# All engines in program order, by unit; integer additions and first own terms on VectorE; round 1's transposes between levels

## The chip, the cores and the metric

One core of one Trainium2 chip. The metric is the device time of one execution in microseconds (us); quoted are medians of all the runs of a kernel, at first with the lowest and highest. One caution on names: SyncE issues the loads, GpSimd appears as POOL in the profile, ScalarE as ACT, VectorE as DVE, TensorE as PE and its weight loads as PEld.

## The reference

A recurrence over 768 time steps for 4 batches and 8 heads of 48 channels, then a normed two-layer MLP with a residual:

```python
for t in range(S):                                   # S = 768, B = 4, H = 8, D = 48
    cur = einsum('bhd,bhe->bhde', u[None] * kt, vt)  # the step's "own term"
    y[:, :, t] = einsum('bhd,bhde->bhe', rt, state + cur)
    state = wt[..., None] * state + einsum('bhd,bhe->bhde', kt, vt)
x  = y transposed to (B, S, H*D)                      # 384 channels
xn = (x - mu) / sqrt(var + 1e-6) * g_ln
out = x + relu(xn @ w_ch1) @ w_ch2                    # 384 -> 1536 -> 384
```

The two weight matrices arrive as 64-bit words and are made into 32-bit floats on the chip.

## The kernel before

The work is cut into eight **rounds** (a batch and half its steps), each of two **units** (four heads). A round's recurrence is done in six **levels**: TensorE makes products (`a_ps`, the quads), VectorE multiplies `r` and `k` by the decays (grow) and keeps blocks under a mask. The MLP of a round runs in 24 steps, spread over the levels of the rounds after it. A level of round 1 or later, with its share of MLP steps, is called a **slot**; slots 0 to 7 are round 1 and two levels of round 2.

The 24 blocks of weights are converted one at a time. ScalarE reads the fetched block twice, VectorE runs three integer instructions and GpSimd adds:

```python
PE, ACT, DVE, POOL, SP = nc.tensor, nc.scalar, nc.vector, nc.gpsimd, nc.sync
def matmul(*args, **kw):                     # only TensorE's order is fixed
    tc.keep_in_program_order(PE.matmul(*args, **kw))

def weights():
    ...
    for i, (dst, _) in enumerate(parts):     # 24 blocks, 3 raw buffers
        fetch(i + 2)                         # SyncE loads 384 KB
        ...
        ACT.activation(out=e.bitcast(F32), in_=hi.bitcast(F32), func=AF.Abs, scale=2.0**-16)
        ACT.activation(out=low, in_=lo, func=AF.Copy, scale=2.0**-29)
        DVE.tensor_scalar(...)               # clamp
        DVE.tensor_scalar(...)               # shift and mask
        DVE.scalar_tensor_tensor(...)        # sign
        POOL.tensor_tensor(out=dst.bitcast(I32), in0=e, in1=low, op=ALU.add)
        yield
```

ScalarE has a second duty: it takes the transposes (`wT`, `kT`, `rT`, `kn`, `xT`) and the MLP's Relu (`h`) out of PSUM, and TensorE waits for it whenever a PSUM buffer is full (two for each of these two kinds). Outside TensorE a scheduler decides where each instruction stands in its engine's queue. The driver:

```python
for rnd in range(1, NR + 1):
    for lev in range(NLEV):
        ...
        if now: level(now, lev)              # quads, grow, keep
        tasks = []                           # transposes of round rnd + 1, ...
        ...
        fill(until, tasks)                   # tasks mixed with the MLP's steps
        ...
        convert(3)                           # three weight blocks a slot, after the slot
```

## Time and profile before

| | before |
|---|---|
| time | 634.4 us, median of 3 (631.36 to 634.47) |
| profiled span | 628.1 us |
| first MLP matmul (`h_ps`) | 85.4 us |
| end of slot 7 | 150.4 us |
| TensorE busy in slots 0 to 7 | 59.45 of 65.0 us, granted clock 0.91 |
| the rest of the span | 477.7 us, TensorE busy 466.16 |

Two lines of the view of waits, cut to 64 to 151 us, matter for what follows. In this view a line names the engine and tile that waited, what it waited for, then the total in us, how often and the longest. These are ScalarE's waits at the two instructions that open a weight block:

```profile
ACT wl L212 <- POOL w_sb L225: 5.5, 1, 5.5
ACT we L209 <- DMA raw<-in_moe_w_ch_dram: 5.1, 6, 1.1
```

On these two lines ScalarE stands for 10.6 us at weight blocks in some 87 us, half of it in one piece for GpSimd's addition; the waits for loads are 1.1 us at the longest. (Ahead of 64 us it waits 21.2 us more for weight loads, before the MLP has begun.)

### The profile page before, as it was taken

What the parts mean: (1) busy time and instruction counts of PE and PEld (TensorE: products, weight loads), DVE (VectorE), ACT (ScalarE), POOL (GpSimd) and SP (SyncE); (2) the same over time, 40 slices, a digit from 0 to 9 for tenths busy, and PEclk for the clock granted to TensorE, in tenths of its full rate; (3) what the DMA queues carried; (4) which work ended last, traced back from release to release, by engine and by line L of the source; (5) the groups of instructions that cost most, each with busy time, mean ns of one, the idle gap of its engine ahead of it and who ended that gap; (6) DMA issues with size and microseconds to landing.
All of it is one profiled execution on the core that took longest, in us unless ns stands there. A gap on an engine that the chain in (4) does not pass through costs nothing.

```text
span 628.1 us, 19238 instructions
## 1 busy us (share of the span) xinstructions
PE 573.4 (91%) x8456; PEld 387.2 (62%) x8456; DVE 303.2 (48%) x683; ACT 185.2 (29%) x402; POOL 152.4 (24%) x205
## 2 busy tenths in 40 slices
PE   5366597989999999999999999999999999999997
PEld 4255465656656766667667666676666666566554
DVE  1598959867563544452646356355226361231000
ACT  4108426352143311531243213331142004301200
POOL 7666737670160013300330005101030000000000
PEclk9556769889999989999999999998999999999999
DMA  7656766803410342013400341002000000000000
GB/s 134 144 105 190 182 124 175 183 14 77 91 48 1 59 94 47 15 39 74 88 15 12 68 99 38 1 16 46 26 15 3 15 15 14 1 15 25 1 13 25
DMA packets 123251, 36.83 MB, mean 59 GB/s; under 512 B 116896, under 2 KB 120096, under 8 KB 123168
## 3 DMA queue, kind: packets, MB, share of 16 engines
q1 hardware_dynamic: 121568, 35.32, 25.4%
q8 instruction: 66, 1.08, 0.7%
q10 hardware_dynamic: 1600, 0.30, 0.3%
q14 instruction: 17, 0.14, 0.1%
HBM read 30.87 MB, written 4.72 MB: 57 GB/s over the span
## 4 chain that ended last, share of the span: by engine, by line
PE 82%; DVE 8%; issue 3%; DMA 2%; POOL 2%; SPq 2%; ACT 1%; POOLq 0%; DVEq 0%; ACTq 0%
PE h_ps L56 30%; PE o_ps L56 29%; PE a_ps L56 10%; PE y L56 4%; PE kv L56 2%; PE r_ps L59 2%; PE kn_ps L59 2%; SPq L112 2%; DVE we L221 1%; PE w_ps L59 1%; PE xT_ps L59 1%; DMA nat_r<-in_r_dram 1%; DVE kT L309 1%; PE k_ps L59 1%; DVE rT L309 1%
## 5 line engine op out<-in xcount | busy, mean ns | idle before, releaser
L56 PE MATMUL h_ps<-xT,w_sb 128*128 128x384 f32 x576 | 202.1, 499 | 2.2 <-ACT h L475 2.2
L56 PE MATMUL o_ps<-w_sb,h 128*128 128x384 f32 x576 | 201.2, 495 | 0.0
L56 PEld LDWEIGHTS h_ps<-xT,w_sb 128*128 128x128 f32 x576 | 107.3, 194 | 66.5 <-issue 4.2
L56 PEld LDWEIGHTS o_ps<-w_sb,h 128*128 128x128 f32 x576 | 106.4, 194 | 61.3 <-issue 3.0
L56 PE MATMUL a_ps<-rT,kT 48*64 48x32 f32 x4608 | 86.8, 229 | 25.8 <-DVE kT L309 20.2
L56 PEld LDWEIGHTS a_ps<-rT,kT 48*64 48x64 f32 x4608 | 81.2, 146 | 37.4 <-issue 19.7
L475 ACT ACTIVATE h<-h_ps 128x384 f32<-128x384 f32 x96 | 47.0, 489 | 114.6 <-PE h_ps L56 111.7
L487 DVE TENSOR_TENSOR o<-o_ps,x 128x384 f32<-128x384 f32 x24 | 13.3, 556 | 118.3 <-PE o_ps L56 118.3
L280 POOL TENSOR_TENSOR vo<-v,own 128x576 f32<-128x576 f32 x16 | 19.5, 1221 | 196.1 <-DMA v<-in_v_dram 123.9
L309 DVE TENSOR_TENSOR kT<-kT,tot 128x384 f32<-128x384 f32 x80 | 60.2, 752 | 0.0
L323 DVE COPY_PREDICATED A<-mask,a_ps 128x384 f32<-128x384 int8 x80 | 54.6, 751 | 0.0
L309 DVE TENSOR_TENSOR rT<-rT,tot 128x384 f32<-128x384 f32 x80 | 49.9, 623 | 4.3 <-PE a_ps L56 2.1
L374 DVE SCALAR_TENSOR_TENSOR s<-s,decay,kv 128x48 f32<-128x48 f32 x160 | 30.4, 258 | 43.7 <-PE kv L56 43.7
L421 DVE TENSOR_TENSOR x<-y,vo 128x576 f32<-128x576 f32 x16 | 12.1, 757 | 61.6 <-PE y L56 61.6
L225 POOL TENSOR_TENSOR w_sb<-we,wl 128x384 int32<-128x384 int32 x24 | 33.7, 1416 | 25.6 <-DVE we L221 22.5
L264 POOL TENSOR_TENSOR rk<-nat_k,nat_r 128x576 f32<-128x576 f32 x16 | 27.1, 1691 | 36.1 <-DMA nat_r<-in_r_dram 17.3
L275 DVE TENSOR_REDUCE own<-rk 128x12 f32<-128x576 f32 x16 | 12.0, 749 | 46.5 <-POOL rk L269 46.5
L460 ACT ACTIVATE xT<-xT_ps,g_sb 128x384 f32<-128x384 f32 x24 | 13.9, 580 | 58.5 <-PE xT_ps L59 58.5
L241 ACT COPY rT<-r_ps 128x384 f32<-128x384 f32 x32 | 14.6, 477 | 50.7 <-PE r_ps L59 50.7
L241 ACT COPY kT<-k_ps 128x384 f32<-128x384 f32 x32 | 14.8, 478 | 43.9 <-PE k_ps L59 43.8
L56 PEld LDWEIGHTS y<-v,A 64*64 64x64 f32 x384 | 21.8, 138 | 8.1 <-issue 7.1
L255 POOL TENSOR_TENSOR tot<-wT 128x384 f32<-128x384 f32 x16 | 14.6, 911 | 46.9 <-DVE kT L309 46.8
(57 smaller groups left out, 591.1 us busy)
## 6 DMA issues: line engine op xcount, KB each, us to landing
raw<-in_moe_w_ch_dram SPq DMA_DIRECT2D x24, 384.0 KB, 3.7
nat_w<-in_w_dram SPq DMA_DIRECT2D x64, 72.0 KB, 2.5
nat_k<-in_k_dram SPq DMA_DIRECT2D x64, 72.0 KB, 2.5
v<-in_v_dram SPq DMA_DIRECT2D x64, 72.0 KB, 2.8
out_dram<-o SPq DMA_DIRECT2D x24, 192.0 KB, 2.0
nat_r<-in_r_dram SPq DMA_DIRECT2D x60, 72.0 KB, 2.4
vx<-in_v_dram SPq DMA_DIRECT2D x64, 36.0 KB, 2.3
nat_r<-in_r_dram ACTq DMA_DIRECT2D x4, 72.0 KB, 3.7
```

The source lines that it names most:

```text
L56: tc.keep_in_program_order(PE.matmul(*args, **kw))
L59: tc.keep_in_program_order(PE.transpose(*args))
L225: POOL.tensor_tensor(out=dst.bitcast(I32), in0=e, in1=low, op=ALU.add)
L241: ACT.copy(out=a[nm][:, ts(pr, RN)], in_=ps)
L255: POOL.tensor_tensor(out=t, in0=pair[:, :, 0], in1=pair[:, :, 1], op=ALU.mult)
L264: POOL.tensor_tensor(out=rk, in0=nat["k"][q % 2][:, :, :, 0:D], in1=nat["r"][q % 2][:, :, :, 0:D], op=ALU.mult,)
L280: POOL.tensor_tensor(out=a["vo"], in0=vn[q], in1=o[:, :, :, None].broadcast_to([P, NH, TT, D]), op=ALU.mult,)
L309: DVE.tensor_tensor(out=X, in0=X, in1=T[:, :, 1 - i][:, :, None].broadcast_to(blocks), op=ALU.mult,)
L323: DVE.copy_predicated(out=out_j[:, :, :, 1, :], mask=mask, data=ps_j)
L374: DVE.scalar_tensor_tensor(out=s[:, pr, m, :], in0=s[:, pr, m - 1, :] if m else before[:, pr, 2 * TT - 1, :], scalar=a["T"][NLEV][:, c : c ...
L460: ACT.activation(out=xTs[rnd][:, kc, :], in_=ps, func=AF.Copy, scale=g_sb[:, kc : kc + 1])
L475: ACT.activation(out=hs[f], in_=ps, func=AF.Relu)
```

## The change

Its intent: let VectorE do what GpSimd slowed it for, start VectorE on unit 0 as soon as that unit has arrived, use TensorE's idle prologue for round 1's transposes, and fix every order by hand, so that the tuned order is what runs. The core of the diff:

```diff
+class InOrder:                       # every call is kept in program order
+    def __getattr__(self, name):
+        ...
+        return lambda *args, **kw: self.tc.keep_in_program_order(f(*args, **kw))
-    PE, ACT, DVE, POOL, SP = nc.tensor, nc.scalar, nc.vector, nc.gpsimd, nc.sync
+    PE, ACT, DVE, POOL = (
+        InOrder(tc, e) for e in (nc.tensor, nc.scalar, nc.vector, nc.gpsimd)
+    )
+    SP = nc.sync
...
+    praw = ctx.enter_context(tc.tile_pool(name="praw", bufs=4))
+    RAW = 4
+    def begin():                         # "opening": ScalarE, needs raw[i] and a low buffer
+        ...
+            low[i] = p3.tile([P, WC], I32, tag="low", name=f"low{i}")     # 3 buffers
+            ACT.activation(out=parts[i][0], in_=hi.bitcast(F32), func=AF.Abs, scale=2.0**-16)
+            ACT.activation(out=low[i], in_=lo, func=AF.Copy, scale=2.0**-29)
+    def join():                          # VectorE, then the freed raw buffer is loaded again
+        ...
-            POOL.tensor_tensor(out=dst.bitcast(I32), in0=e, in1=low, op=ALU.add)
+            DVE.tensor_tensor(out=bits, in0=bits, in1=low.pop(i), op=ALU.add)
+            joined = i + 1
+            fetch()
...
+    for lev in range(1, NLEV):           # round 0
+        for q in (u0, u1):
+            quads(q, lev)
+        if lev > 1:
+            run(ahead[3 * lev - 6 : 3 * lev - 3])     # round 1's transposes
...
+    states(u1)
+    begin()
+    begin()
+    exchanged(u1)
...
+    PARTS = (2, 2, 2, 3, 3, 3, 3, 3)
...
+            if slot < len(PARTS):
+                for _ in range(PARTS[slot]):
+                    tasks += [join, begin]            # ahead of the slot's transposes
...
+            fill(until, tasks)
```

An **opening** is ScalarE's two reads of a block, into the weight tile and a `low` buffer; a **join** is VectorE's four instructions that finish the block, after which its raw buffer is loaded again. The own terms of the first four units and their products of decays (`totals`) go to VectorE, and VectorE's copies of `x` before the norm are gone. At the start of the MLP six blocks are open and three joined.

## The prediction

> **What bounds the kernel now.** I read the page's slices first, then the busy times in three windows of my own, the groups by line, and the timeline of VectorE. The slices show two regimes. In the first five or so of 40, TensorE is about half busy and its granted clock is low; from about the ninth on it is 90% busy or more at a clock of 0.8 to 1.0.
>
> ```profile
> PE   5366597989999999999999999999999999999997
> DVE  1598959867563544452646356355226361231000
> PEclk9556769889999989999999999998999999999999
> ```
>
> The windows put numbers on it. I cut at 85.40 us, where the first MLP matmul (`h_ps`) starts, and at 150.40, where the second level of round 2 ends. Columns: length, then busy time of PE, PEld, DVE, ACT, POOL, then clock and DMA.
>
> ```profile
> 0.00:85.40 85.40, 47.81 (x1038) 39.45 (x1038) 58.31 (x119) 33.31 (x70) 55.33 (x87) 0.67 0.68 151
> 85.40:150.40 65.00, 59.45 (x930) 39.73 (x930) 51.15 (x104) 30.32 (x68) 36.38 (x32) 0.91 0.48 111
> 150.40:628.10 477.70, 466.16 (x6490) 308.01 (x6489) 193.70 (x460) 121.54 (x264) 60.70 (x86) 0.99 0.16 35
> ```
>
> The last 477.7 us have 11.5 us of idle TensorE, and 3.4 of those belong to the tail after 560 us. Its work is the same in both kernels, so little can be won there. Of the first 85.4 us TensorE is idle for 37.6. From 25 to 50 us VectorE was busy for all 25.00 us: it is the bound of the prologue (round 0, before the first MLP). In the middle window TensorE lacks 5.5 us. So a change of the schedule can move only two dates: when the first MLP starts, and when TensorE reaches the end of the eighth slot. A slot is one level of rounds 1 and later with its share of MLP steps; slots 0 to 7 are round 1 and two levels of round 2. At the end of slot 7 both kernels have issued 17 of the 24 steps of the first MLP, since the formula for the steps is the same.
>
> The groups show what makes VectorE slow:
>
> ```profile
> L225 POOL TENSOR_TENSOR w_sb<-we,wl 128x384 int32<-128x384 int32 x24 | 33.7, 1416 | 25.6 <-DVE we L221 22.5
> L309 DVE TENSOR_TENSOR kT<-kT,tot 128x384 f32<-128x384 f32 x80 | 60.2, 752 | 0.0
> L323 DVE COPY_PREDICATED A<-mask,a_ps 128x384 f32<-128x384 int8 x80 | 54.6, 751 | 0.0
> ```
>
> and the timeline of VectorE, then of GpSimd, shows the same instruction at two speeds:
>
> ```profile
> 54.50 0.36 DVE L217 TENSOR_SCALAR we<-we 128x384 int32<-128x384 int32 x1
> 54.90 0.56 DVE L221 SCALAR_TENSOR_TENSOR we<-raw,we 128x384 int32<-128x384 int32 x1
> 57.83 1.00 DVE L217 TENSOR_SCALAR we<-we 128x384 int32<-128x384 int32 x1
> 57.60 1.00 POOL L225 TENSOR_TENSOR w_sb<-we,wl 128x384 int32<-128x384 int32 x1 [1.00 <-DVE we L221]
> ```
>
> L217 takes 0.36 us alone and 1.00 beside GpSimd's addition.
>
> **What the Trainium skill says.** "GPSIMD Engine Reference", section "Key points": GpSimd shares its SBUF interfaces with VectorE and contends with instructions in a two-port mode or with two SBUF inputs. The trace agrees (0.36 against 1.00). Its section "Engine selection" puts two-input elementwise work on VectorE, GpSimd being about twice slower: here 1.416 us for 384 integers against 0.55 for a float product of that size on VectorE. "VectorE: DVE Perf Modes", section "Specifications", says that VectorE converts integers and is exact only below 2^24. The added integers are 31-bit patterns; the listing of the changed program shows each addition as one custom instruction over 768 half-words, so the sum is kept exact some other way, and no row of this trace times it. "TensorE: Matmul & The Clock Gate", Part 1, says that the clock is half until TensorE has been busy for some microseconds. The slices agree that it is low in the prologue (0.50 from 25 to 50 us at 63% busy); a weaker clock there matters only if TensorE becomes the bound.
>
> **The change part by part.** Durations are rows of this trace without GpSimd beside them; independent instructions of 384 elements start 0.47 us apart though each lasts 0.55.
>
> *Moved to VectorE.* 24 additions: I take 0.55 to 0.6 each (0.95 if it handles one half-word in the time of a float). A whole conversion (`join`) is now a chain of dependent instructions, 0.36 + 0.36 + 0.56 + 0.6 plus gaps of 0.03: 1.9 us, for 24 of them 45.6. Before, the three instructions cost 0.698 + 0.496 + 0.491 = 1.69 with contention. The own terms of the first four units: two products of 576 (0.75, as L421 takes) and a reduction (0.75): 2.3 each, 9.2; then four scalings 0.75: 3.0. Their `totals`, six dependent products from 384 down to 12 elements: I estimate 1.8 each, 7.2.
>
> *Stays on VectorE, up to the end of slot 7.* 14 levels: 56 products x 0.47 = 26.3; kept blocks 0.94 each in levels 0 and 1 (1.88 for two at 27.02 us), six levels x 2: 11.3; 0.52 in levels 2 to 4, 12 of them: 6.2. States 44 x 0.2 = 9; outputs, moments and norm 5.2; two reductions for round 2: 1.5. Sum of all: 45.6 + 9.2 + 3.0 + 7.2 + 26.3 + 11.3 + 6.2 + 9 + 5.2 + 1.5 = 124.5 us.
>
> *Removed.* GpSimd's load of 55 + 36 us up to 150 us falls to the set-up of masks and round 2's terms. Over the first 160 us the excess of VectorE's durations over their fast forms is about 25 us (6.9 in L323, 8.7 in the L309 rows, 9.9 in the three conversion rows): most of it goes. Three copies of `x` per round (0.35 each) go too, off the path.
>
> *The first date.* The own terms no longer hold the levels back: before, the first level waited for GpSimd's `rk` and `vo`, and VectorE's first product came at 24.1 us. Now unit 0's data (here by 8 us) and unit 1's (14 us) start VectorE at about 8, and level 0 is kept by 21. Levels 1 to 5 with one join, 18 us: 39. Totals, two joins, states, terms, outputs, moments, norm, 20 us: 59. The MLP starts at 60 to 64 instead of 85.4, about 23 us earlier. Round 1's transposes, set between levels, fill TensorE's idle time there (its rows: 0.8 us for three at the low clock, 0.43 at the full one).
>
> *The second date.* In before 12 of the 24 conversions fell before the MLP; now only 3 do, and 21 lie in slots 0 to 7. A slot costs VectorE 6.7 to 11.6 us and TensorE 5.7 to 9. VectorE becomes the bound there: 8 + 124.5 + about 5 of waits (unit 1's load, cold TensorE, round trips) + 3 of contention with round 2's GpSimd work = 140.5. Step 16 of the MLP needs the last weights; it, the transposes and step 17 add about 4: TensorE is through slot 7 at 144.5, against 150.4. So 23 us won in the prologue shrink to 6. In the last window I give 2.5 more for fewer waits (at 106 to 111, 152 to 155 and 173 to 181 us in before, two of them after 150). Together 8.5.
>
> **The rivals.** (1) *VectorE's conversions eat all*: with 0.95 us for an addition the ledger grows by 24 x 0.35 = 8.4 and the gain is zero, about 634; 640 if waits come on top. For it: the 768 half-words. Against it: VectorE need not read them one by one. (2) *The prologue's gain lasts*: if the chains overlap better than my 1.9, or the MLP's steps lean less on the last joins, half of the 23 us remains: 634 - 15 = 619, at best 608. For it: a schedule that names every order was surely made so that TensorE is fed. (3) *Head-of-line waits*: with each engine in program order a late weight or input stops everything behind it. The load queue asks for four weight blocks of 384 KB before round 1's inputs, and TensorE would stand before their transposes in the middle of the levels. DMA runs at 0.6 to 0.78 already in the prologue. Cost: 3 to 8 us, partly behind VectorE's work. (4) *The gain is hidden*: TensorE's total work is untouched, so nothing under 573 us plus a start is possible.
>
> **Range and chances.** My ledger gives 634.4 - 8.5 = 626. I shade it to 624, since rival 2 seems likelier to me than 1. One standard error of the ledger is near 9 us, from the addition (8), the prologue waits (4) and the chains (4). 2% faster is 621.7, just under my figure: 0.41. Slower than 647 would need rivals 1 and 3 together: 0.05.
>
> **What would show it.** Right: first `h_ps` at 60 to 64 us; L225's counterpart on VectorE at 0.55 to 0.6; products and kept blocks near 0.55 to 0.6 on average in the first 140 us; VectorE over 90% busy from 20 to 140 us, TensorE 70 to 80% in 62 to 140; GpSimd nearly idle from 12 to 90. The last 477 us nearly as before. Wrong: an addition of 0.95; a first MLP after 70 us with TensorE waiting for `nat` or `raw`; or TensorE through slot 7 before 138 us. Then my sizes of the chain, or the thought that VectorE binds the slots, failed.

## The result, and the profile after

The changed kernel takes 664.99 us (660.18 to 666.9, 4 runs) against 632.88 (628.29 to 634.47, 4 runs) for the kernel before on the same chip; the outputs are correct. The ratio is 1.0508 with a 95% interval of 1.0427 to 1.059. Ratios here and below are the mean time of one kernel's fast runs over that of the other's fast runs of the same rounds, so not quite the ratio of the medians. It is 5% slower, where a gain was predicted.

The slices of the changed kernel's page, to be read against the three lines of before in the prediction:

```profile
PE   6897385547689999999999999999999999999997
DVE  4878975446635534335252625353444543202000
PEclk9665796767589999999999989999999999999999
```

The prologue is shorter, but from the fifth to the eleventh slice, where before TensorE was soon at 9, both TensorE and VectorE are half idle and the granted clock is low. The windows, cut at the first `h_ps` and the end of slot 7 (columns: window, length, then busy time of PE, PEld, DVE, ACT, POOL, then clock, DMA share, GB/s):

```profile
0.00:64.66 64.66, 49.86 (x1037) 41.21 (x1038) 48.96 (x124) 26.24 (x55) 9.84 (x37) 0.72 0.66 133
64.66:183.69 119.03, 71.45 (x932) 45.30 (x931) 76.09 (x157) 38.90 (x83) 15.75 (x20) 0.74 0.40 97
183.69:663.10 479.41, 466.94 (x6490) 308.74 (x6489) 177.29 (x455) 122.50 (x264) 65.02 (x88) 0.99 0.16 35
```

The first MLP matmul comes 20.7 us earlier (64.66 against 85.4). The last window is 479.4 us long, against 477.7. So the whole loss lies in slots 0 to 7: 119.0 us in place of 65.0. Some lengthening was planned, since 21 conversions now fall there in place of 12. TensorE does the same work there (932 matmuls against 930), and the 54.0 us fall into two parts. Its idle time is 119.03 - 71.45 = 47.6 us against 65.00 - 59.45 = 5.5, so 42.0 more. The same matmuls keep it busy 71.45 - 59.45 = 12.0 us longer, at a clock of 0.74 in place of 0.91. Loss and gain give 54.0 - 20.7 + 1.7 = 35.0, which is the difference of the spans (663.1 - 628.1).

VectorE got what it was meant to get. The groups of the page (count, then total busy and mean ns, then the idle time ahead and what ended it):

```profile
L48 DVE COPY_PREDICATED A<-mask,a_ps 128x384 f32<-128x384 int8 x80 | 54.3, 748 | 0.0
L48 DVE TENSOR_TENSOR kT<-kT,tot 128x384 f32<-128x384 f32 x80 | 44.2, 552 | 13.7 <-PE a_ps L48 13.6
```

and the groups of VectorE from 0 to 140 us alone, for the addition:

```profile
L48 DVE CUSTOM_DVE_ANT_0 w_sb<-w_sb,low 128x768 uint16<-128x768 uint16 x18 | 11.0, 612 | 2.1
```

A product of `kT` takes 552 ns (752 before), and the addition 0.61 us on average, 0.56 where nothing else slows it. Only the kept blocks stay as they were (748 against 751). But VectorE now waits for TensorE's quads: 13.7 us ahead of the `kT` group, where it never had to before.

What stops? The waits from 64 to 184 us:

```profile
ACT w_sb L48 <- DMA raw<-in_moe_w_ch_dram: 27.2, 13, 10.1
ACT low L48 <- DVE w_sb L48: 26.9, 6, 7.6
...
PE r_ps L48 <- ACT rT L48: 10.1, 1, 10.1
PE h_ps L48 <- ACT h L48: 10.1, 2, 9.3
...
PE o_ps L48 <- DVE w_sb L48: 9.8, 6, 4.9
...
PE w_ps L48 <- ACT wT L48: 8.9, 1, 8.9
...
PE k_ps L48 <- ACT kT L48: 8.6, 1, 8.6
```

ScalarE stands 54.1 us at weight openings (27.2 + 26.9), against 10.6 in the shorter window of before. TensorE's four big stops, 36.9 of its 47.6 idle us, all name ScalarE's copies out of PSUM (`rT`, `h`, `wT`, `kT`), which are half a microsecond long and stand *behind* those openings in ScalarE's queue. Another 9.8 us are six waits of `o_ps` for late joins. The chain of work that ended last, from 100 to 119 us (start, length, what), shows one turn of the loop:

```profile
100.47 0.57 DVE w_sb L48
...
101.10 3.00 DMA raw<-in_moe_w_ch_dram
...
104.12 0.54 ACT w_sb L48
...
105.09 0.38 ACT wT L48
...
105.52 1.54 PE w_ps L48 x6
107.06 3.41 PE h_ps L48 x6
110.46 0.88 PE a_ps L48 x48
...
111.36 0.56 DVE rT L48
...
117.57 0.57 DVE w_sb L48
...
118.19 3.40 DMA raw<-in_moe_w_ch_dram
```

Read it as a ring. A join on VectorE frees a raw buffer; the load lands 3.0 us later; only then can ScalarE open the block, and only then copy `wT`; that lets TensorE go on with transposes, MLP and the next quads; only on those can VectorE grow and keep the next level; and behind those stand its next joins, of which one frees the next buffer. The next load starts 17.1 us after the last one (118.19 - 101.10). Before, TensorE needed some 8 us for a slot. ScalarE's timeline shows the ring's other thread, the `low` buffers (three of them, for up to three joins a slot):

```profile
110.89 0.54 ACT L48 ACTIVATE w_sb<-raw 128x384 f32<-128x384 f32 x1
116.91 0.56 ACT L48 ACTIVATE low<-raw 128x384 int32<-128x384 uint32 x1 [5.48 <-DVE w_sb L48]
119.60 0.56 ACT L48 ACTIVATE w_sb<-raw 128x384 f32<-128x384 f32 x1 [2.13 <-DMA raw<-in_moe_w_ch_dram]
...
122.87 0.85 ACT L48 COPY kT<-k_ps 128x384 f32<-128x384 f32 x2
```

From 111.4 us on ScalarE waits 5.48 us for a `low` buffer that VectorE's first join of the same slot frees, then for a raw block, and the copies of `kT` come at 122.87; TensorE stands still for 8.6 us up to 123.39. One of the four stops is not a turn of this ring: the first (`h_ps`, 9.3 us, up to 82.97) waits for a block whose request left SyncE only at 77.84, behind loads of inputs. TensorE's timeline shows the second part of the loss too:

```profile
71.51 2.20 PE L48 MATMUL h_ps<-xT,w_sb 128*128 128x384 f32 x6 [0.85 <-ACT h L48]
82.97 3.69 PE L48 MATMUL h_ps<-xT,w_sb 128*128 128x384 f32 x6 [9.26 <-ACT h L48]
```

Six matmuls that take 2.20 us otherwise take 3.69 after a stop of 9.26 us.

### The profile page after: what moved, and what is told of

Read it like the earlier page. It is cut to its first block, busy times and chain, and to the rows that moved or that the text cites. A ratio compares the mean times of both kernels' runs of the same rounds, so it can differ in the third digit from the quotient of the medians.

```text
span 663.1 us, 19182 instructions
## 1 busy us (share of the span) xinstructions
PE 588.2 (89%) x8456; PEld 395.3 (60%) x8456; DVE 302.3 (46%) x735; ACT 187.6 (28%) x402; POOL 90.6 (14%) x145
## 4 chain that ended last, share of the span: by engine, by line
PE 80%; DVE 9%; DMA 4%; SPq 3%; issue 2%; ACT 2%; ACTq 0%; DVEq 0%
PE o_ps L48 28%; PE h_ps L48 27%; PE a_ps L48 10%; DVE w_sb L48 4%; PE y L48 3%; DMA raw<-in_moe_w_ch_dram 2%; PE kv L48 2%; PE w_ps L48 2%; PE k_ps L48 2%; PE r_ps L48 2%; PE kn_ps L48 2%; PE xT_ps L48 2%; SPq L123 2%; DVE A L48 1%; DMA nat_r<-in_r_dram 1%
## 5 line engine op out<-in xcount | busy, mean ns | idle before, releaser
L48 PE MATMUL o_ps<-w_sb,h 128*128 128x384 f32 x576 | 206.7, 505 | 9.8 <-DVE w_sb L48 9.8
L48 PE MATMUL h_ps<-xT,w_sb 128*128 128x384 f32 x576 | 199.8, 499 | 10.1 <-ACT h L48 10.1
L48 DVE TENSOR_TENSOR o<-o_ps,x 128x384 f32<-128x384 f32 x24 | 13.4, 556 | 140.5 <-PE o_ps L48 140.5
L48 POOL TENSOR_TENSOR vo<-v,own 128x576 f32<-128x576 f32 x12 | 13.9, 1156 | 341.4 <-DVE own L48 341.4
L48 DVE TENSOR_TENSOR rT<-rT,tot 128x384 f32<-128x384 f32 x80 | 43.6, 553 | 21.5 <-PE a_ps L48 16.0
L48 DVE TENSOR_TENSOR kT<-kT,tot 128x384 f32<-128x384 f32 x80 | 44.2, 552 | 13.7 <-PE a_ps L48 13.6
L48 DVE TENSOR_TENSOR x<-y,vo 128x288 f32<-128x288 f32 x32 | 13.1, 452 | 65.7 <-PE y L48 65.7
L48 PE MATMUL w_ps<-ident,nat_w 128*128 128x128 f32 x96 | 19.2, 342 | 14.4 <-ACT wT L48 8.9
L48 PE MATMUL r_ps<-ident,nat_r 128*128 128x128 f32 x96 | 18.9, 333 | 10.4 <-ACT rT L48 10.4
L48 PE MATMUL k_ps<-ident,nat_k 128*128 128x128 f32 x96 | 19.3, 334 | 9.7 <-ACT kT L48 8.6
L48 PE MATMUL y<-sx,rx 48*64 48x48 f32 x384 | 26.0, 228 | 1.4 <-ACT sx L48 1.2
```

What stands on the lines that cost most here:

```text
L48: return lambda *args, **kw: self.tc.keep_in_program_order(f(*args, **kw))
```

## The experiments

The theory: with ScalarE in program order, an opening that needs a buffer freed by a join of the same slot holds up the copies behind it, and the ring above follows. Rivals: the work moved to VectorE is the cost; the order of the load queue is; or program order costs round trips wherever the openings stand. The chips differ from job to job; each ratio is to the kernel before on the same chip. The rows of `before` and of the changed kernel are those of the result.

| run | edit to | median us | ratio [95%] | first `h_ps`, end of slot 7 |
|---|---|---|---|---|
| before | | 632.88 | | 85.4, 150.4 |
| changed kernel | before | 664.99 | 1.051 [1.043, 1.059] | 64.7, 183.7 |
| lead1 | changed | 648.67 | 1.026 [1.020, 1.032] | 64.7, 170.2 |
| lead0 | changed | 646.1 | 1.022 [1.016, 1.029] | 64.8, 169.9 |
| lead0_low4 | changed | 639.35 | 1.013 [1.006, 1.020] | 63.7, 159.4 |
| actfree | changed | 646.37 | 1.022 [1.016, 1.028] | 71.1, 166.7 |
| wlast | changed | 639.06 | 1.010 [1.003, 1.018] | 64.5, 159.0 |
| wlast_sporder | changed | 640.68 | 1.013 [1.005, 1.021] | 63.7, 161.3 |
| sporder | changed | 662.6 | 1.049 [1.042, 1.057] | 65.3, 183.1 |
| addpool | changed | 658.43 | 1.040 [1.033, 1.047] | 64.1, 179.5 |
| peonly | changed | 635.81 | 1.009 [1.003, 1.015] | 67.9, 154.1 |
| split | changed | 628.83 | 0.996 [0.990, 1.001] | 65.1, 152.5 |
| splitfirst | changed | 625.44 | 0.991 [0.986, 0.996] | 64.0, 148.5 |
| splitfirst_sporder | changed | 626.94 | 0.991 [0.984, 0.998] | 63.7, 147.2 |
| split_pool | changed | 625.45 | 0.992 [0.987, 0.997] | 63.9, 147.2 |
| split_loads | changed | 635.25 | 1.005 [0.999, 1.010] | 64.4, 156.7 |
| before_inorder | before | 668.77 | 1.057 [1.051, 1.063] | 100.3, 176.2 |
| before_add_own | before | 626.07 | 0.992 [0.985, 0.999] | 89.4, 149.9 |
| before_aot | before | 627.58 | 0.995 [0.989, 1.000] | 91.4, 155.5 |

### Which part of the change loses

**before_inorder**: the kernel before with ScalarE, VectorE and GpSimd in program order, nothing else.

```diff
-    PE, ACT, DVE, POOL, SP = nc.tensor, nc.scalar, nc.vector, nc.gpsimd, nc.sync
+    PE, SP = nc.tensor, nc.sync
+    ACT, DVE, POOL = (InOrder(tc, e) for e in (nc.scalar, nc.vector, nc.gpsimd))
```

> The kernel before with ScalarE, VectorE and GpSimd in program order, and nothing else of the change (TensorE was in order already). Ring: a conversion asks its three engines in turn, so a block that has not landed stops VectorE and ScalarE with all that follows: slower than before by 8 to 40 us, 640 to 672. If program order by itself does no harm and the work moved to VectorE is the cause: within 6 us of before, 627 to 639.

Measured 668.77, 1.057. Program order alone, on the text of before, costs as much as the whole change. The place is another one: the first `h_ps` slips to 100.3 us, and TensorE's waits from 20 to 180 us are led by

```profile
PE a_ps L70 <- DVE kT L48: 39.0, 8, 10.4
```

so here it is VectorE's queue that makes TensorE wait. VectorE's own longest waits there are for GpSimd's product `rk` (37.8 us in 5 pieces), which the reduction of an own term needs, and all that stands behind it is held up. This shows that program order can lose this much; it does not by itself show the ring.

**before_add_own**: the kernel before with the additions and the first four units' own products and terms on VectorE, placed by the scheduler.

```diff
-            POOL.tensor_tensor(out=dst.bitcast(I32), in0=e, in1=low, op=ALU.add)
+            DVE.tensor_tensor(out=dst.bitcast(I32), in0=e, in1=low, op=ALU.add)
-    def own_term(q):
+    def own_term(q, eng=POOL):           # and its three POOL products by eng
-        own_term(q)
+        own_term(q, DVE)                 # for rounds 0 and 1
```

> The kernel before with only the second part of the change: the 24 integer additions and the own terms of the first four units on VectorE, placed by the scheduler. Ring: this work is not the cause; VectorE gets 24 x 0.6 + 4 x 2.25 + 4 x 0.75 = 26 us more, and loses about 20 of its 25 us of contention with GpSimd: 628 to 642. Rival 1 (VectorE too full): 648 to 665.

Measured 626.07, ratio 0.992 with the interval below 1. The moved work is not the loss; by itself, placed by the scheduler, it gains a little (0.1 to 1.5%).

**addpool**: the changed kernel with the 24 additions back on GpSimd.

```diff
-            DVE.tensor_tensor(out=bits, in0=bits, in1=low.pop(i), op=ALU.add)
+            POOL.tensor_tensor(out=bits, in0=bits, in1=low.pop(i), op=ALU.add)
```

> The changed kernel with only the 24 integer additions put back on GpSimd. Ring: the additions are not the cause; each slot loses about 2 us of VectorE's work, but the opening now waits for GpSimd's addition, 1.0 to 1.4 us: 652 to 670. Rival 1 (VectorE too full with the additions, 24 x 0.6 us = 14 us plus what queues behind): 635 to 648.

Measured 658.43: about 1% back, and the end of slot 7 only 4 us earlier. The stops stay: ScalarE then waits for the `low` buffer at GpSimd instead (27.5 us from 60 to 160 us). The additions are not the main cause.

**sporder**: the load queue in program order as well.

```diff
-    SP = nc.sync
+    SP = InOrder(tc, nc.sync)
```

> The changed kernel with the load queue (SyncE) in program order as well; it was the one queue left to the scheduler, which moves loads of v, vx and later inputs ahead of weight block 7 (issued at 77.84 us, asked for at 70). Ring: the first stop of ScalarE (10.1 us up to 81.56) goes, the later ones, each waiting for a block fetched in the same slot, stay: 650 to 658. Rival 2 (late blocks by the queue's order are the whole cause): 628 to 640. Rival 1 (VectorE too full): no change, 660 to 667.

Measured 662.6, within the interval of the changed kernel and not the 650 to 658 that the theory expected. The first stop shrank to 7.1 us of TensorE and did not go: in program order, too, twelve input loads (68.90 to 76.37 us) stand ahead of that block's request. So this other order of the loads changes nothing; a queue without inputs ahead of the blocks was not tried on the changed kernel.

**before_aot**: before_add_own with the third part of the change as well, round 1's loads at level 0 and its transposes between levels 2 to 5 of round 0; the scheduler still places the other engines.

```diff
-        if lev == 1:
             for q in new:
                 load(q)
+        if lev > 1:
+            for task in ahead[3 * lev - 6 : 3 * lev - 3]:
+                task()
...                                      # and taken out behind round 0's levels
```

> The kernel before with the additions and the first four units' own terms on VectorE (that alone measured 0.992 of the kernel before) and also with round 1's loads at level 0 and its transposes between levels 2 and 5 of round 0; the scheduler places ScalarE, VectorE and GpSimd. If TensorE's idle time in the prologue can take those transposes, the MLP starts some 5 us earlier and the time is 616 to 624. If they only stand in TensorE's queue before levels that VectorE sets, or wait for late inputs, 624 to 632.

Measured 627.58, in the second of the two ranges: the first `h_ps` comes at 91.4, not earlier. Transposes between the levels give nothing where the scheduler places the rest.

### Which queue, and what in it

**actfree** sets ScalarE alone free, **peonly** frees ScalarE, VectorE and GpSimd.

```diff
-    PE, ACT, DVE, POOL = (
-        InOrder(tc, e) for e in (nc.tensor, nc.scalar, nc.vector, nc.gpsimd)
+    PE, DVE, POOL = (
+        InOrder(tc, e) for e in (nc.tensor, nc.vector, nc.gpsimd)
     )
-    SP = nc.sync
+    ACT, SP = nc.scalar, nc.sync
```

> The changed kernel with program order dropped on ScalarE alone, so that the scheduler places its instructions. Ring: copies and activations that TensorE waits for can pass a weight opening that is not ready; 625 to 645, TensorE's waits for rT, kT, wT and h (10.4, 8.6, 8.9, 10.1 us) fall to under 10 in all. Rival 1 (VectorE too full): 660 to 667, the same. Rival 2 (late blocks): 655 or more.

```diff
+    PE = InOrder(tc, nc.tensor)
+    ACT, DVE, POOL, SP = nc.scalar, nc.vector, nc.gpsimd, nc.sync
```

> The changed kernel's text with program order kept for TensorE alone, as the kernel before has it; ScalarE, VectorE, GpSimd and SyncE are placed by the scheduler. If program order of the other three engines makes the whole loss, the eighth slot ends before 150 us and the time is 612 to 632, at or under the kernel before. If the changed placement itself (round 1's transposes between levels, only three blocks joined ahead of the MLP) costs as well, the time stays above 640 as it does with ScalarE alone set free (646).

actfree gives 646.37, just over its range of 625 to 645: of the 5.1% it takes back 2.9. The sign named for it came true: TensorE's waits for `rT`, `kT`, `wT` and `h` fall from 37.7 to about 3 us. peonly gives 635.81, 1.009, between the two ranges that were expected (612 to 632, above 640). So program order of ScalarE, VectorE and GpSimd together is worth 4 of the 5%; with ScalarE alone freed, TensorE's waits that stay (64 to 184 us) are for VectorE: 21.1 us of `o_ps` and `h_ps` for late joins and one of 8.8 for the norm (`xn`). That they come from VectorE's fixed order is likely, since peonly frees it, but VectorE alone was not set free.

**lead1** removes two of the three openings that the change adds late in the prologue, **lead0** all three, and **lead0_low4** gives `low` a fourth buffer besides. In each, every other call keeps its place in the text.

```diff
     states(u1)
-    begin()
-    begin()
     exchanged(u1)
```

> The changed kernel with two calls of begin taken out of the prologue, so that ScalarE opens weight block i+1 rather than i+3 when block i has been joined; the work is the same. Theory (ring): in every slot ScalarE stands at an opening that waits for a block fetched two microseconds earlier, or for a low buffer that the same slot's join frees, and the copies that TensorE needs queue behind it. Then the 27 us and 27 us of ScalarE's waits for raw and low mostly vanish, slots 0 to 7 shrink from 119 us to some 80 to 88, and the time is 625 to 636. Rival 1 (VectorE is too full with the additions): no change, 660 to 667. Rival 2 (the DMA queue delivers the blocks late whatever the order): 650 or more, with ScalarE or VectorE still waiting for raw.

```diff
     states(u1)
-    begin()
-    begin()
     exchanged(u1)
...
     run(each(turned_x, [0], range(KC)))
-    begin()
     mlps.append(mlp(0))
```

> The changed kernel with only the lead taken away: the last three openings ahead of the first MLP are removed, so that an opening needs the block asked for three joins earlier in place of one of the same slot, and its low buffer is the one freed two joins before. The order of tasks in a slot (join, opening, join, opening in front of the transposes) stays. Head-of-line theory: the waits of ScalarE for raw and low shrink as in split, but each opening stands between the copies and each join right behind its opening, so a part of the loss stays: 630 to 645, under lead1's 649. Rival (where the joins stand makes the loss, not what the openings wait for): no better than lead1, 645 to 655.

```diff
+    pl = ctx.enter_context(tc.tile_pool(name="pl", bufs=4))
-            low[i] = p3.tile([P, WC], I32, tag="low", name=f"low{i}")
+            low[i] = pl.tile([P, WC], I32, tag="low", name=f"low{i}")
```

> lead0 with four low buffers in place of three, nothing else. In lead0's trace ScalarE still waited 16.7 us (4 times) for a low buffer: with joins and openings taken in turn, the last opening of a slot takes the buffer that the slot's first join frees. With four it takes one freed in the slot before. Theory (what an opening waits for makes the stops, more than where it stands): the waits for low fall under 4 us and the time falls to 630 to 640. Rival (the place of joins and openings among the transposes makes the stops): 643 to 650, as lead0.

The fewer blocks are open in advance, the older the buffer that an opening needs. lead1 gains 2.5%, less than expected (648.67 for 625 to 636; slots 0 to 7 take 105.5 us, not 80 to 88): ScalarE's waits for `low` and raw fall to 16.8 and 8.6 us but do not vanish. lead0 missed its range (646.1 for 630 to 645): it is no better than lead1, and by the text the rival won. But it was hardly another kernel: `join()` opens its block itself when none is open, so from the first slot on lead0 issues the same order as lead1, with one block open in advance, and the two timelines of ScalarE agree within half a microsecond up to 97 us. The waits of lead0 from 64 to 160 us are those of lead1 too:

```profile
ACT low L48 <- DVE w_sb L48: 16.7, 4, 5.9
...
ACT w_sb L48 <- DMA raw<-in_moe_w_ch_dram: 8.5, 3, 5.9
```

My reading of its buffers was wrong. Joins and openings alternate, so the last opening of a slot of three takes the `low` buffer that the first join of the same slot frees: that dependence was still there. lead0_low4 removes it and nothing else. It gives 639.35, in the theory's range, the end of slot 7 comes 10.5 us earlier, and ScalarE's waits for `low` are gone. (The intervals of the two ratios, from different chips, overlap a little.) In both kernels the instructions stand in the same order; only what an opening waits for has changed. That part of the theory is shown. A part of the wait has only moved: ScalarE now stands longer for loads than in lead0, 19.5 us in place of 8.5, since a raw block is still asked for shortly before it is needed:

```profile
ACT w_sb L48 <- DMA raw<-in_moe_w_ch_dram: 19.5, 7, 6.3
```

More raw buffers would be the direct test. No run has them (four take 12 KB of each partition). That is left open.

### Where the openings stand

**wlast** moves each slot's joins and openings behind its other tasks; **wlast_sporder** adds program order of the loads.

```diff
-            if slot < len(PARTS):
-                for _ in range(PARTS[slot]):
-                    tasks += [join, begin]
             if rnd > 1 and lev == 0:
...
                 tasks += each(totals, new, [POOL])
+            if slot < len(PARTS):
+                for _ in range(PARTS[slot]):
+                    tasks += [join, begin]
             fill(until, tasks)
```

> The changed kernel with the weights' tasks of each slot moved behind its transposes, instead of ahead of them. Ring: the transposes' copies leave ScalarE before it stands at a weight opening, so TensorE waits less inside the slot; but MLP activations are still mixed with the openings: 628 to 650. Rival 1 and rival 2: 655 to 667.

> Weights behind the transposes in each slot, and the load queue in program order. Ring and queue order add up: the slots come down to VectorE's own ledger, so TensorE is through slot 7 at 146 to 152 us and the time is 625 to 634. If something else holds the slots: 636 or more, as with the weights last alone (639).

wlast gains 25 us of the 33 at the end of slot 7, to 639.06: the copies no longer stand behind openings of their own slot. One stop of 7.7 us of `h_ps` and 10.6 us of `o_ps` waiting for late conversions remain. Program order of the loads again changes nothing (640.68, where 625 to 634 was expected if the two added up).

**split** and **splitfirst** undo the ring: no block is open when the MLP starts, a slot opens its three blocks (in split behind the transposes, in splitfirst ahead of them) and joins them at its end. Their raw blocks were then asked for one slot earlier, and all three `low` buffers are free.

```diff
-    PARTS = (2, 2, 2, 3, 3, 3, 3, 3)
+    PARTS = (3, 3, 3, 3, 3, 3, 3)
...
-            if slot < len(PARTS):
-                for _ in range(PARTS[slot]):
-                    tasks += [join, begin]
...
+            if slot < len(PARTS):
+                tasks = [begin] * PARTS[slot] + tasks + [join] * PARTS[slot]   # splitfirst
+                # split: tasks += [begin] * PARTS[slot] + [join] * PARTS[slot]
             fill(until, tasks)
```

(The three openings late in the prologue are removed as in lead0.)

> The changed kernel, still with every engine in program order, but with slack put into the weights' ring: the MLP starts with no opened block, each of slots 0 to 6 opens its three blocks on ScalarE behind the slot's transposes and joins them on VectorE at the end of the slot. So all three raw blocks were fetched one slot earlier and all three low buffers are free when ScalarE reaches an opening. Head-of-line theory (ScalarE's queue stands at an opening whose block or buffer only a join of the same slot frees): ScalarE's waits for raw and for low nearly vanish in slots 0 to 7 (below 8 us together, against 54), the eighth slot ends near 150 us instead of 184, time 625 to 640. Rival (program order costs round trips between TensorE and VectorE wherever the openings stand; the ring is only where the waits happen to be booked): the waits move to other pairs, the eighth slot ends after 165, time above 645.

> As split, but the slot's three openings stand ahead of the slot's transposes, where the changed kernel had its first one; the joins stay at the slot's end. Their blocks were asked for at the end of the slot before, so they may land late. Head-of-line theory: an opening early in the queue is harmless if its block has landed; with a landing of 3 to 4 us after the join of the slot before, a part of the waits for raw returns, in front of the transposes' copies; the time lies between split and the version with the weights last (639), some 630 to 645. Rival: the same as split within 0.5%, since only the number of round trips counts.

split takes 628.83 and ends slot 7 at 152.5; splitfirst takes 625.44 and ends it at 148.5. All engines are still in program order and the same work is done, so it isn't program order as such that costs 5%, but what stands behind what in it. The theory's main figures hold (625 to 640, near 150), with two misses. The waits for raw shrank to 18.0 and 21.6 us from 64 to 150 us, not under 8 together. And splitfirst was expected slower than split; the two agree within 0.5%, as the rival had it: an opening ahead of the transposes does little harm once its block is on the way (`w_ps` waits once behind `wT`, 5.9 us). The window of slots 0 to 7 in splitfirst, columns as before:

```profile
63.99:148.46 84.47, 62.84 (x931) 42.01 (x931) 75.48 (x156) 39.68 (x87) 17.05 (x20) 0.84 0.54 136
```

In slots 0 to 7 VectorE is busy for 75.48 of 84.47 us, 89%; in the changed kernel it was 76.09 of 119.03. With most stops gone VectorE is the bound there, as predicted. TensorE's same 931 matmuls cost 62.84 us at a clock of 0.84. Against the changed kernel that is 8.6 us less of busy time and 26.0 less of idle time (47.6 - 21.6).

### The stop that remains

In split and splitfirst one long wait of ScalarE is left (9.6 us, 71 to 80 us in splitfirst). SyncE's issues in that stretch (start, length, queue, what):

```profile
66.61 4.58 SPq L138 DMA_DIRECT2D vx<-in_v_dram  x7
71.28 3.08 SPq L123 DMA_DIRECT2D nat_k<-in_k_dram  x4
...
76.69 2.50 SPq L208 DMA_DIRECT2D raw<-in_moe_w_ch_dram  x3
```

The block's load goes out at 76.69, behind inputs of rounds 1 and 2. Three runs tried it: **splitfirst_sporder** (loads in program order), **split_loads** (and those inputs put behind the joins) and **split_pool** (splitfirst with GpSimd issuing all blocks after the fourth).

```diff
-            SP.dma_start(                              # split_pool
+            (SP if i < RAW else POOL).dma_start(
...
-    for q in new:                                      # split_loads, with SP in order
-        load_v(q)
-        load_vx(q)
-                tasks += each(load, new[lev : lev + 1])
+            if rnd == 1 and lev < 2:                   # after the slot's joins
+                tasks += each(load_v, now[lev : lev + 1]) + each(load, new[lev : lev + 1])
+                tasks += each(load_vx, now[lev : lev + 1])
```

> splitfirst with the load queue in program order too. In splitfirst one stop is left: ScalarE stands 9.6 us (from 70.9 to 80.5) at the opening of the block that was asked for at 76.7 us, behind some 25 loads of rounds 1 and 2 that the scheduler put ahead of it. If the order of the loads in the queue makes that stop, program order (the eight blocks' requests stand behind round 1's v loads here as well, but ahead of the second unit's) shortens it to 3 to 6 us: 620 to 625. If the queue's order doesn't matter, as it did not in the changed kernel and with the weights last, the same as splitfirst within 0.5%, 624 to 629.

> splitfirst with all weight blocks after the first four asked for by GpSimd, which is idle there, at the join that frees the buffer, so that they no longer stand behind the inputs' loads in SyncE's queue. If the queue's order makes the stop that is left (9.6 us on ScalarE at 71 to 80 us), the request goes out near 69 us, ScalarE's waits for raw fall from 21.6 to under 8 us, the eighth slot ends 4 to 7 us earlier (142 to 145) and the time is 617 to 622. If the transfer bandwidth or round 1's inputs, now sharing it, hold TensorE instead, 623 to 629 as splitfirst.

> splitfirst_sporder with round 1's v loads and round 2's first inputs put behind the joins of slots 0 and 1 in the load queue, so that the weights' blocks are asked for as soon as a join frees a buffer. If the one stop that splitfirst keeps (9.6 us on ScalarE, about 8 on TensorE) comes from the queue, it falls under 3 us and the time is 614 to 621, the eighth slot ending near 142. If the loads then come late for the own terms and the second round's transposes, or DMA bandwidth is the limit, 622 to 630.

None beats splitfirst. In splitfirst_sporder the wait falls to 7.8 us and the time is the same (626.94). In split_pool the one long stop is gone, but the waits for raw are still 21.0 us in 12 pieces of at most 3.6, and slot 7 ends at 147.2, 1.3 us earlier, not 4 to 7. What holds it now, the window from 64 to 100 us shows (columns as above):

```profile
64.00:100.00 36.00, 25.91 (x346) 16.76 (x346) 33.77 (x69) 16.96 (x36) 5.36 (x10) 0.83 0.68 162
```

VectorE is busy 33.77 of 36 us. There is little left to win from waits once VectorE is that full. split_loads is 1.4% slower than splitfirst_sporder of the same job, and over both of its ranges (614 to 621, 622 to 630). It moved the stop to the next slots: the inputs put behind the joins of slots 0 and 1 stand, in program order, ahead of the blocks that the joins of slots 1 and 2 ask for. Slot 2's first join had freed its raw buffer by about 92.4 us, but the request went out at 100.43, behind the 20 input loads from 87.62 on; ScalarE stood 10.2 us for that block, and TensorE 10.1 behind `wT`. So the place of inputs in the load queue does cost time here.

The best versions, splitfirst (0.991) and before_add_own (0.992), beat the kernel before by a little under 1%; the 2% mark was not reached.

## Why the prediction was wrong

**Right: most of the sizes.** The first `h_ps` was put at 60 to 64 us and came at 64.66, just outside. The addition was put at 0.55 to 0.6 us and takes 0.56 alone, 0.61 on average. VectorE's own ledger up to the end of slot 7 was 124.5 us of work; measured are 48.96 + 76.09 = 125.05. GpSimd's part fell from 55.33 to 9.84 us in the prologue, and the products from 752 to 552 ns. Rival 1 (a slow addition) is out. Two small ones were wrong. The kept blocks were put near 0.55 to 0.6 us on average and stayed at 0.75; the prediction's own sum had 0.94 for levels 0 and 1 and 0.52 for the next three, and these are what the trace shows (1.86 and 1.02 us for two), so only the sign contradicted the sum. The last window was put 2.5 us shorter and is 1.7 us longer.

**Wrong: the step "VectorE becomes the bound there", with "about 5 of waits".** It was a sum of one engine's work with a small allowance, 140.5 us, and 4 for TensorE's tail: 144.5. The signs named for it failed too: VectorE was to be over 90% busy from 20 to 140 us and TensorE 70 to 80% from 62 to 140, and they were busy 90.67 of 120 and 42.48 of 78 us, 76 and 54%. In the changed kernel VectorE had the predicted work, but by 183.69 us it had been without work for 183.69 - 125.05 = 58.6 us, where the sum allowed 20 (8 of start, 5, 3 and 4). In splitfirst the same difference is 148.46 - (49.09 + 75.48) = 23.9 us. In the changed kernel no engine was the bound: the stops in ScalarE's queue were, most of them turns of the ring.

**Wrong: the size of rival 3.** Head-of-line waits were named, but at 3 to 8 us "partly behind VectorE's work", and tied to the load queue and to the transposes' inputs. The prediction's own dates leave 144.5 - 62 = 82.5 us for slots 0 to 7; splitfirst takes 84.5 there and the changed kernel 119.0. So they cost some 35 us, and stood at ScalarE, in front of PSUM copies and Relu. sporder and the first stop show that the load queue has a small part in it, not the main one. The chance of 0.05 for a time over 647 rested on rivals 1 and 3 together; rival 3 at its true size was enough. The step missed was to follow each opening back to the join that frees its buffer, and to ask whether that join stands behind work that this opening holds up. The Trainium skill has the fact in "PSUM — Partial Sum Buffer", section "Engine vs sequencer instructions": "ScalarE/VectorE/GpSimdE queues are strict FIFO." The trace agrees: a `wT` copy of half a microsecond came out only after the openings ahead of it, and TensorE stood 8.9 us.

**Wrong: that a weak clock "matters only if TensorE becomes the bound".** Six matmuls took 3.69 us after a stop and 2.20 otherwise (granted clock 0.59 and 1.00 in these two stretches), and in slots 0 to 7 the same matmuls took 12.0 us longer than before. "TensorE: Matmul & The Clock Gate", Part 1, says that the clock falls back to half after an idle window of about 3.4 us; the trace agrees in that the long stops are followed by slow matmuls and a window at 0.74. TensorE's slowness is on the path here: its matmuls are links of the chain shown above (`h_ps`, 3.41 us). Undoing the stops took back 8.6 of the 12.0 us.

**What the repaired order says of the ledger.** splitfirst, with the same work on each engine and the ring undone, ends slot 7 at 148.5 for the predicted 144.5 and takes 625.4 us for the predicted 624. The arithmetic described an order of instructions that the changed kernel did not have. That the prologue's 21 us shrink to a few in slots 0 to 7 came out as the prediction said, since the conversions then fall there.

**Still open:** how much of the changed kernel's loss is ScalarE's ring and how much VectorE's fixed order (actfree leaves 2.2%, lead0_low4 1.3%, split nothing clear of noise): VectorE was never set free alone, and more raw buffers were not tried.

## What to carry to other kernels

When an engine's order is fixed by hand, list for each instruction that waits for a buffer which instruction frees it, and what stands behind the waiter; if the freer depends on something behind the waiter, even by way of three engines, the order is a ring and each turn costs the sum of all its latencies. Open work only when its buffers were freed a stage earlier, or put the openings behind what others wait for: that was worth 26 to 40 us here (wlast, splitfirst). One more `low` buffer alone was worth some 7, and moving the additions and own terms to a faster engine some 5. A ledger of busy time bounds a schedule from below only; before trusting it, check the dependences through the queues.

## What the Trainium skill lacked or had wrong

- "GPSIMD Engine Reference", section 4.1, gives the exact 32-bit integer addition for GpSimd, and "VectorE: DVE Perf Modes", section "Specifications", says that VectorE is exact only below 2^24. The runs show the 31-bit addition on VectorE with correct outputs, as one custom instruction over 128x768 half-words of 0.56 us alone; on GpSimd it took 1.416 us on average. Neither page has it. (Each half-word is below 2^24, so the limit on the page is not contradicted.)
- "PSUM — Partial Sum Buffer" states the strict FIFO queues, but I found no page that tells what it costs when a queue's head waits for a buffer freed further round a loop: here 17.1 us for one turn in place of a slot of some 8, and the larger part of the 5.1% of the kernel (splitfirst takes back all of it).
